# Turning the first batch's K, Q and P on TensorE instead of on VectorE and by DMA

## The chip, the cores and the metric

The kernel runs on one core of a Trainium2 chip. The metric is device time in microseconds for one execution, taken as the median of several runs. The profile is one execution, recorded by the hardware profiler. Engines are named as in the profile: PE is TensorE, PEld its weight loads, DVE is VectorE, ACT is ScalarE, POOL is GpSimd, SP is SyncE, which here only issues transfers.

## What is computed

Block-causal attention over 8 batches, 8 heads, 576 positions and 64 channels a head, and then a feed-forward layer on the 4608 rows of 512 values.

```python
scores = scale * np.matmul(q, k.transpose(0, 1, 3, 2))
mask = block_i >= block_j          # blocks of 64 positions
scores = np.where(mask, scores, -1000000000.0)
attn = np.exp(scores - np.max(scores, axis=-1, keepdims=True))
attn = attn / (np.sum(attn, axis=-1, keepdims=True) + 1e-09)
x = np.matmul(attn, v)             # then heads side by side: 4608 x 512
h = np.maximum(np.maximum(x @ w1, x @ w2), x @ w3)   # 512 -> 768
return h @ w_out                                     # 768 -> 512
```

All of it is in float32.

## The kernel before

Attention works by pairs of heads (class `Pair`, four pairs a batch, with two `Head` objects each). The feed-forward layer works by chunks (class `Chunk`): a batch's 576 rows are cut in half 0 (256) and half 1 (320). Its products at line 919 use operands split in a high and a low part of type fp32r, three products for one; the weights are split the same way on the chip. Class `Unit` does that for one weight block of 512 columns: 24 units, each with a transfer issued by POOL, two ScalarE passes (L288 and a cast in the helper at L235), five VectorE passes (`clamp` L294, `shift` L301, `sign` L307, `power` L313, `rest` L324), three products (L331, which is fp32 and shows as two records, L332 and L333), and a last copy.

The first batch is treated apart, so that the feed-forward layer can begin early. It is cut in FRONT pairs, which take queries and keys 0 to 255 (tiles t = 0 and 1 of 128 queries), and BACK pairs, which take queries 256 to 575 (tiles 2 and 3, and the last 64 queries of both heads together as tile 4) against all 576 keys. Later batches use EARLY and WHOLE pairs, with all queries. For a tile t the scores are 128 x 128(t+1).

For one pair the steps are these. `load` fetches K on SP's queue and Q on ScalarE's (SP's in later batches) into the tile `nat`, in four transfers each that put 32x32 blocks where a 32x32 turn wants them (L709). `turn_qk` turns them on VectorE into `kq` (L730 for FRONT, L733 for the others). `qk` makes the scores in PSUM (L749; `qk4` at L756 for tile 4). `top` takes the minimum of the negated scores on VectorE (L406), `exp` the exponential on ScalarE (L499; `exp4` L773), `scale` divides by the sum, on ScalarE (L422) or GpSimd (L424). P must then be turned, as P·V contracts over the keys. `turn` does it by 32x32 blocks on VectorE into `pz` (L522, and L526 for the rest of tile 4), and `move` sends the four quarters of partitions to their place in `pt` by four transfers on SP's queue (L534). `exp` writes in an order that suits this (`by_turns`). `pv` multiplies (L801), and the result is copied (the helper `copy`, L235 on ScalarE, L237 on VectorE) and split in `xh` and `xl` (L240).

The order of all instructions is written out ahead by a planner, `in_order`: every step is a `Job` with a cost on the engines that may do it, a rank, the jobs that it follows and the slots of buffers that it takes and gives back. Each engine takes the ready job of least rank. PSUM tiles named "sb" have five slots, shared by scores and P·V; those named "pm" have three, for the weight conversion and the feed-forward layer.

Of the kernel before, what the change touches and what calls it, by code (L numbers as in the profile page):

```python
# [34 lines left out]
SEND = 620.0  # L35
# [5 lines left out]

GAP = 60.0
SMALL = 130.0
DEBUG = False


class Job:

    def __init__(self, cost, rank, call, after=(), take=(), give=(), lasts=0.0):
        self.cost, self.rank, self.call, self.lasts = cost, rank, call, lasts
        self.take, self.give = list(take), list(give)
        self.next, self.left = [], 0
        for j in after:
            if j is not None:
                j.next.append(self)
                self.left += 1


def in_order(jobs, slots):


    free = {}
    busy = {e: False for e in LAG}
    ready = {e: [] for e in LAG}
    events, seq, out = [], 0, []

    def post(t, kind, job, eng=None):
        nonlocal seq  # L70
        seq += 1
        heapq.heappush(events, (t, seq, kind, job, eng))

    def arrive(t, job, by=None):
        for e in job.cost:
            post(t + (LAG[by][e] if by else 0.0), "ready", job, e)
        if not job.cost:
            post(t + job.lasts, "done", job)

    for n, job in enumerate(jobs):  # L80
        job.n, job.begun = n, False
        if job.left == 0:
            arrive(0.0, job)
    while events:
        t = events[0][0]
        while events and events[0][0] <= t:
            _, _, kind, job, eng = heapq.heappop(events)
            if kind == "ready":
                heapq.heappush(ready[eng], (job.rank, job.n))
            elif kind == "idle":  # L90
                busy[eng] = False
            else:
                for s in job.give:
                    free[s] = free.get(s, slots[s]) + 1
                for nxt in job.next:
                    nxt.left -= 1
                    if nxt.left == 0:
                        arrive(t, nxt, eng)
        for eng, queue in ready.items():
            if busy[eng]:  # L100
                continue
            later = []
            while queue:
                top = heapq.heappop(queue)
                job = jobs[top[1]]
                if job.begun:
                    continue
                if all(free.get(s, slots[s]) >= job.take.count(s) for s in job.take):
                    for s in job.take:
                        free[s] = free.get(s, slots[s]) - 1  # L110
                    job.begun = busy[eng] = True
                    out.append((job, eng))
                    post(t + job.cost[eng], "idle", None, eng)
                    post(t + max(job.cost[eng], job.lasts), "done", job, eng)
# [28 lines left out]
def kernel(  # L143
# [76 lines left out]

    nat = const.tile([P, 2, S], F32, name="nat")

    jobs = []

    def job(cost, rank, call, *args, after=(), take=(), give=(), lasts=0.0):
        j = Job(cost, rank, lambda eng: call(eng, *args), after, take, give, lasts)
        jobs.append(j)
        return j

# [13 lines left out]
    class Unit:  # L243


        def __init__(self, u, src, dst, n, prior, *early, first=None):
# [14 lines left out]
            j = job({}, 0, lambda eng: None, after=(j,), lasts=MOVE)  # L261
# [122 lines left out]
    class Part:  # L384


        def __init__(self, first, later, halves, keys, queries, run, beside=False):
# [7 lines left out]
            self.loads = 1 if keys < S else 2  # L395

    WHOLE = Part(((3,), (2, 0)), (1,), (1, 0), S, slice(0, S), slice(0, RUN), True)
# [28 lines left out]
    class Head:  # L426
# [28 lines left out]
        def turns(self, t0, after):  # L455

            pair, part, self.scales = self.pair, self.pair.part, {}
            for t in part.tiles:
                r = t0 + 8 + t / 2 + (SECOND if part.beside and t in part.later else 0)
                self.scales[t] = job(norm_cost(P * (t + 1)), r, self.scale, t, after=(self.inv[t],))  # L460
            scales, alone = self.scales, part.loads == 2
            self.turned, first = [], None
            if part.last:
# [15 lines left out]
            if alone or self.j:  # L479
                turned = self.turned if alone else self.turned + pair.heads[0].turned  # L480
                self.moved = job(
                    {"SP": 4 * SEND}, t0 + 13, self.move, after=turned, take=("pt",), give=("pz",), lasts=4 * SEND + TURNED
                )
                if not alone:
                    pair.heads[0].moved = self.moved
            return first

        def top(self, eng, t):

# [48 lines left out]
    class Pair:  # L538
# [3 lines left out]
        def __init__(self, b, hp, part, n):  # L542
            self.b, self.hp, self.part = b, hp, part
            self.heads = [Head(self, j) for j in range(2)]
            self.x32, self.o, self.xs, self.ps, self.began = [None, None], {}, {0: [], 1: []}, {}, None

            self.at = 256 * (n % 2) if part.loads == 1 else 0
            self.vn, self.q8 = vns[n % 2].rearrange("p (c h d) -> p c h d", h=2, d=D), q8s[n % 2]

        def plan(self, first, before):  # L550

            part, loads = self.part, {}
            for nm, n, r in (("kn", 4, -15), ("qn", 4, -15), ("vn", 3, -4)):
                e = "ACT" if nm == "qn" and not part.beside else "SP"
                prior = before and before.loads[nm]
                loads[nm] = job(
# [4 lines left out]
                    after=(prior,),  # L561
                    take=(nm,) * (part.loads if nm != "vn" else 1),
                    lasts=n * LOAD + DMA,
                )
            begun.append(loads["kn"])
            n = part.queries.stop - part.queries.start
            tq = job(
                {"DVE": dve(part.keys + n)},
                first - TURN,
                self.turn_qk,  # L570
                after=(loads["kn"], loads["qn"]),
                take=("kq",),
                give=("kn", "qn") * part.loads,
            )

            cost = {ts: 4 * pe(*[P * (t + 1) for t in ts], least=64) for ts in part.groups}
            prior = job(
# [48 lines left out]
            if part.last:  # L626
# [34 lines left out]
        def alone(self, first):  # L661
# [7 lines left out]
                )  # L669
            self.finish(prior, first, priors)  # L670

        def finish(self, prior, r, priors={}):
            self.xjobs = {}
            for half in self.part.halves:
# [14 lines left out]
            join((prior,), ("pt",) * self.part.loads + ("vn",))  # L689

        def values(self, eng):
            for half in self.part.halves:
# [6 lines left out]
        def load(self, eng, nm):  # L699
            src = {"qn": q, "kn": k, "vn": v}[nm]  # L700
            h0 = 2 * self.hp
            if nm != "vn":

                queue = nc.scalar if eng == "ACT" else nc.sync
# [63 lines left out]

        def exp4(self, eng):
            nm, sm, _ = self.stat  # L770
            self.p4 = att.tile([P, S], F32, name="p4", bufs=slots["p4"])
            for a in range(2):
                nc.scalar.activation(  # L773
                    by_turns(self.p4[:, self.of4(a)], False),
                    by_turns(self.ps[a], True),
                    AF.Exp,
                    bias=nm[:, 1:2],
                    scale=-1.0,
# [9 lines left out]
        def inverse4(self, eng):  # L788
            rs = self.stat[2]
            nc.vector.reciprocal(rs[:, 0:1], rs[:, 0:1])  # L790

        def scale4(self, eng):
            normalise(eng, self.p4, self.stat[2][:, 0:1])

        def pv(self, eng, half):

# [282 lines left out]
```

## Time and profile before

| | us |
|---|---|
| median of 3 runs | 936.66 (935.87 to 937.34) |
| the profiled execution, its own time | 936.99 |
| its span | 935.2 |
| TensorE busy | 884.5 |
| VectorE busy | 537.4 |
| ScalarE busy | 469.4 |
| GpSimd busy | 252.0 |

A busy time is the union of an engine's instructions; a releaser in the profile is the instruction that ended a wait, as semaphore events tell it. The granted clock is a share of TensorE's full 2.4 GHz; its lower level is 1.2 GHz, so a stretch at 0.75 is half at the one and half at the other. The span is shorter than the execution by what lies before the first and behind the last instruction, here 1.8 us.

### The profile page before, as it was taken

What the parts mean: (1) busy time and instruction counts of PE and PEld (TensorE: products, weight loads), DVE (VectorE), ACT (ScalarE), POOL (GpSimd) and SP (SyncE); (2) the same over time, 40 slices, a digit from 0 to 9 for tenths busy, and PEclk for the clock granted to TensorE, in tenths of its full rate; (3) what the DMA queues carried; (4) which work ended last, traced back from release to release, by engine and by line L of the source; (5) the groups of instructions that cost most, each with busy time, mean ns of one, the idle gap of its engine ahead of it and who ended that gap; (6) DMA issues with size and microseconds to landing.
All of it is one profiled execution on the core that took longest, in us unless ns stands there. A gap on an engine that the chain in (4) does not pass through costs nothing.

```text
span 935.2 us, 16716 instructions
## 1 busy us (share of the span) xinstructions
PE 884.5 (95%) x5736; PEld 730.2 (78%) x5736; DVE 537.4 (57%) x1571; ACT 469.4 (50%) x1332; POOL 252.0 (27%) x376
## 2 busy tenths in 40 slices
PE   3578987999999999999999999999999999999998
PEld 2246754787787888888888888888888888899997
DVE  5596988687763646556564645565574655431111
ACT  3474565575554554647455555556364555422111
POOL 4342322234322231313231232214131222222201
PEclk9798999999999999999999999999999999999999
DMA  6794455876555555545435555555533553320010
GB/s 137 200 307 95 113 134 137 169 161 138 124 110 127 110 132 109 110 112 117 104 67 128 109 120 109 128 110 123 115 79 88 111 125 81 96 72 24 1 34 23
DMA packets 244693, 104.92 MB, mean 112 GB/s; under 512 B 202112, under 2 KB 236928, under 8 KB 244608
## 3 DMA queue, kind: packets, MB, share of 16 engines
q1 hardware_dynamic: 221952, 88.91, 42.3%
q0 software_dynamic: 3456, 12.58, 4.2%
q10 hardware_dynamic: 19200, 2.36, 1.6%
q8 instruction: 45, 0.74, 0.3%
q14 instruction: 40, 0.33, 0.1%
HBM read 41.94 MB, written 9.44 MB: 55 GB/s over the span
## 4 chain that ended last, share of the span: by engine, by line
PE 86%; DMA 5%; DVE 5%; ACT 2%; issue 1%; SPq 1%; ACTq 0%; DVEq 0%
PE pm L919 48%; PE pm L985 16%; PE sb L801 10%; PE sb L749 8%; PE sb L756 3%; DMA pt<-pz 2%; DMA nat<-in_q_dram 2%; PE pm L331 1%; DVE pz L522 1%; ACT p L499 1%; DMA vn<-in_v_dram 1%; SPq L534 1%; DVE left L324 1%; DVE sb L406 1%; DMA nat<-in_k_dram 0%
## 5 line engine op out<-in xcount | busy, mean ns | idle before, releaser
L919 PE MATMUL pm<-xh,w 128*128 128x320 f32 (+1 forms) x2304 | 496.9, 303 | 2.7 <-ACT w L235 2.1
L919 PEld LDWEIGHTS pm<-xh,w 128*128 128x128 f32 x2304 | 378.5, 190 | 22.5 <-issue 14.1
L919 PE MATMUL pm<-xl,w 128*128 128x256 f32 (+1 forms) x1152 | 340.9, 296 | 1.8 <-POOL xl L240 1.8
L919 PEld LDWEIGHTS pm<-xl,w 128*128 128x128 f32 x1152 | 218.6, 190 | 8.0 <-issue 4.8
L406 DVE CUSTOM_DVE_ANT_0 sb<-sb,mask 128x512 f32<-128x512 f32 (+3 forms) x288 | 144.6, 527 | 124.1 <-PE sb L756 68.9
L934 DVE TENSOR_TENSOR m<-pm,m 128x256 f32<-128x256 f32 (+1 forms) x192 | 87.0, 453 | 163.6 <-PE pm L919 155.3
L522 DVE STREAM_TRANSPOSE pz<-p 128x384 f32<-128x384 f32 (+3 forms) x320 | 156.9, 525 | 21.3 <-ACT p L422 18.1
L499 ACT ACTIVATE p<-sb,nm 128x128 f32<-128x128 f32 (+3 forms) x256 | 134.3, 528 | 67.3 <-DVE nm L406 58.4
L240 POOL TENSOR_TENSOR hl<-m,hh 128x256 fp32r<-128x256 f32 x96 | 71.2, 741 | 320.6 <-ACT hh L235 288.9
L424 POOL TENSOR_TENSOR p<-p,rs 128x384 f32<-128x384 f32 (+4 forms) x132 | 97.8, 762 | 187.2 <-DVE rs L637 174.2
L801 PE MATMUL sb<-pt,vn 128*64 128x320 f32 (+4 forms) x896 | 105.6, 379 | 19.1 <-DMA pt<-pz 16.8
L985 PE MATMUL pm<-wo,hh 128*128 128x512 f32 x384 | 119.9, 392 | 0.9 <-ACT wo L235 0.9
L801 PEld LDWEIGHTS sb<-pt,vn 128*64 128x64 f32 x896 | 63.0, 143 | 60.4 <-issue 19.1
L749 PE MATMUL sb<-kq 64*128 64x256 f32 (+3 forms) x512 | 91.3, 476 | 15.6 <-DVE kq L730 12.5
L235 ACT CAST hh<-m 128x256 fp32r<-128x256 f32 x96 | 38.9, 406 | 124.1 <-DVE m L934 119.2
L422 ACT ACTIVATE p<-p,rs 128x512 f32<-128x512 f32 (+4 forms) x156 | 86.3, 599 | 20.9 <-DVE rs L637 12.3
L240 POOL TENSOR_TENSOR xl<-x,xh 128x256 fp32r<-128x256 f32 (+1 forms) x64 | 51.4, 808 | 156.8 <-ACT xh L235 156.8
L749 PEld LDWEIGHTS sb<-kq 64*128 64x128 f32 x512 | 46.9, 196 | 51.0 <-issue 20.8
L985 PEld LDWEIGHTS pm<-wo,hh 128*128 128x128 f32 x384 | 70.9, 188 | 16.1 <-ACT wo L235 1.7
L985 PE MATMUL pm<-wo,hl 128*128 128x512 f32 x192 | 74.8, 390 | 0.0
L235 ACT COPY m<-pm 128x256 f32<-128x256 f32 (+1 forms) x96 | 38.3, 399 | 41.5 <-PE pm L919 27.8
L235 ACT COPY osb<-pm 128x512 f32<-128x512 f32 x36 | 21.1, 587 | 71.3 <-PE pm L985 71.3
(68 smaller groups left out, 683.6 us busy)
## 6 DMA issues: line engine op xcount, KB each, us to landing
pt<-pz SPq DMA_DIRECT2D x224, 200.0 KB, 4.0
w<-in_moe_w_dram POOLq DMA_DIRECT2D x18, 512.0 KB, 6.9
nat<-in_k_dram SPq DMA_DIRECT2D x128, 72.0 KB, 2.4
vn<-in_v_dram SPq DMA_DIRECT2D x64, 128.0 KB, 2.4
out_dram<-osb SPq DMA_DIRECT2D x32, 256.0 KB, 2.0
nat<-in_q_dram SPq DMA_DIRECT2D x96, 72.0 KB, 2.6
pt<-pz SPq DMA_DIRECT2D x32, 152.0 KB, 4.4
wo<-in_moe_w_out_dram POOLq DMA_DIRECT2D x6, 512.0 KB, 4.4
```

The costliest lines, as they stand in the source:

```text
L235: nc.scalar.copy(dst, src)
L240: {"DVE": nc.vector, "POOL": nc.gpsimd}[eng].tensor_tensor(out=dst, in0=a, in1=b, op=ALU.subtract)
L406: nc.vector.tensor_tensor_reduce(out=ps, in0=ps, in1=hidden, scale=-SCALE, scalar=first, op0=ALU.add, op1=ALU.min, accum_out=out_)
L422: nc.scalar.mul(p, p, r)
L424: nc.gpsimd.tensor_tensor(out=p, in0=p, in1=r.broadcast_to([P, p.shape[1]]), op=ALU.mult)
L499: nc.scalar.activation(by_turns(self.p[t], False), by_turns(self.ps.pop(t), True), AF.Exp, bias=nm[:, c : c + 1], scale=-1.0, accum_out=sm ...
L522: nc.vector.transpose(dst, p[:, 0 : n * P])
L749: nc.tensor.matmul(ps, self.q[h.own, P * t : P * (t + 1)], self.k[h.own, 0:w], start=True, stop=True)
L801: nc.tensor.matmul(o[h.own].rearrange("p (i u) -> p i u", u=n)[:, :, c0 : c0 + z - a], self.vn[:, kt, h.j, :], h.pt[:, :, h.off + a : h.of ...
L919: nc.tensor.matmul(self.ps, w[i, f][:, c, :], xx, start=(c == 0 and s == 0), stop=(c == NC - 1 and s == 2))
L934: nc.vector.tensor_tensor(out=m, in0=ps, in1=m, op=ALU.max)
L985: nc.tensor.matmul(self.po[: self.rows], h, w[f], start=(f == 0 and s == 0), stop=(f == NF - 1 and s == 2))
```

## The change

For FRONT and BACK pairs, which are the first batch alone, the turns go to TensorE. `load` fetches K and Q in natural order (position on the partition, both heads' channels side by side in a run of 128 columns, so runs of 64 floats) into 128x128 chunks of the same tile `nat`: two transfers for 128-row chunks of the two heads, and a third for the last 64 positions. `raise_qk` turns each chunk by a 128x128 transpose on TensorE into an "sb" tile of PSUM, and `place_qk` copies from there into `kq`, on ScalarE or VectorE as the planner picks. For P, `exp` writes in natural order, `raise_p` (and `raise4` for tile 4, whose last 64 columns GpSimd first copies beside themselves) turns by the same transpose, and `place` and `place4` copy into `pt` in the order that `pv` reads. No `pz` and no `move` is left in the first batch. The later batches keep their steps.

The planner gets a new property of a job, `moved`: the time that its transfer takes on a single DMA resource, which the planner fills in sequence (`landing`). It is given to the weight loads, to K, Q and V, and to the moves, of all batches; so orders may differ in the later batches as well.

```diff
+RAISE = 215.0
...
-    FRONT = Part(((1, 0),), (), (0,), 256, slice(0, 256), slice(0, 96))
-    BACK = Part(((3,), (2,)), (), (1,), S, slice(256, S), slice(96, RUN))
+    FRONT = Part(((1, 0),), (), (0,), 256, slice(0, 256), slice(0, 96), plain=True)
+    BACK = Part(((3,), (2,)), (), (1,), S, slice(256, S), slice(96, RUN), plain=True)
...
+            if part.plain:
+                return self.plain_turns(t0)
...
+        def plain_turns(self, t0):
+            pair, part = self.pair, self.pair.part
+            heads = pair.heads
+            shared = part.loads == 1 and self.j
+            gate = heads[0].gate if shared else None
+            first = heads[0].placed[0] if shared else None
+            self.placed = []
+            def place(call, *args, n, after):
+                j = job(
+                    {"ACT": act(n), "DVE": dve(n)},
+                    t0 + 12,
+                    call,
+                    *args,
+                    after=(after, first or (self.placed[0] if self.placed else None)),
+                )
+                self.placed.append(j)
+                return j
+            for t in part.tiles:
+                up = job(
+                    {"PE": RAISE * (t + 1)},
+                    t0 + 12,
+                    self.raise_p,
+                    t,
+                    after=(self.scales[t], gate),
+                    take=("sb",) if gate else ("sb", pair.tag),
+                )
+                gate = self.gate = gate or up
+                join((up,), (f"p{t}",))
+                join((place(self.place, t, n=P * (t + 1), after=up),), ("sb",))
+            if part.last:
+                if self.j == 0:
+                    pair.raised = [
+                        job({"PE": RAISE * n}, t0 + 12, pair.raise4, a, after=(pair.scaled, gate), take=("sb",))
+                        for a, n in ((0, 4), (1, 1))
+                    ]
+                    join(pair.raised, ("p4",))
+                for a, n in ((0, 256), (1, 64)):
+                    place(self.place4, a, n=n, after=pair.raised[a])
+                if self.j == 1:
+                    for a in range(2):
+                        join([h.placed[-2 + a] for h in heads], ("sb",))
+            self.moved = join(self.placed, ())
+            self.first = None
+            return None
+        def raise_p(self, eng, t):
+            p = self.p[t]
+            z = psa.tile([P, P * (t + 1)], F32, name="sb")
+            for c in range(t + 1):
+                nc.tensor.transpose(z[:, c * P : c * P + P], p[:, c * P : c * P + P], plus.bitcast(F32))
+            self.ps[t] = z
...
+        def place(self, eng, t):
+            a, step, u = PLACE[t]
+            n = t + 1
+            a += self.off + u + 32 - step
+            dst = self.turned_p()[:, :, a : a + step * n].rearrange("p i (k u) -> p k i u", u=step)[:, :, :, step - 32 :]
+            copy(eng, dst, self.ps.pop(t).rearrange("p (k i c) -> p k i c", i=4, c=32))
...
+            dst, src = self.p[t], self.ps.pop(t)
+            if not self.pair.part.plain:
+                dst, src = by_turns(dst, False), by_turns(src, True)
             nc.scalar.activation(
-                by_turns(self.p[t], False), by_turns(self.ps.pop(t), True), AF.Exp, bias=nm[:, c : c + 1], scale=-1.0, accum_out=sm[:, c : c + 1]
+                dst, src, AF.Exp, bias=nm[:, c : c + 1], scale=-1.0, accum_out=sm[:, c : c + 1]
             )
...
+            if part.plain:
+                tq = self.plain_qk(first - TURN, loads)
+            else:
...
+        def plain_qk(self, rank, loads):
+            part, o = self.part, self.at // P
+            if part.loads == 1:
+                banks = ((((o, o + 1, 4 + o, 5 + o), ((0, 0, 256),)),))
+            else:
+                a = part.queries.start // P
+                own = tuple(range(a, 4))
+                banks = [((4, 5, 6, 7), ((0, 2, 512),))]
+                if a:
+                    banks.append(((*own, 8), ((0, 1, P * len(own)), (P * len(own), 0, 64))))
+                else:
+                    banks += [(own, ((0, 1, 512),)), ((8,), ((0, 0, 64),))]
+            ups, downs = [], []
+            for n, (chunks, copies) in enumerate(banks):
+                up = job(
+                    {"PE": RAISE * len(chunks)},
+                    rank,
+                    self.raise_qk,
+                    n,
+                    chunks,
+                    after=(loads["kn"], loads["qn"]),
+                    take=("sb", "sb5") + (("kq",) if n == 0 else ()),
+                ) if n == 0 else job(
+                    {"PE": RAISE * len(chunks)}, rank, self.raise_qk, n, chunks, after=(ups[0], loads["kn"], loads["qn"]), take=("sb", "sb5")
+                )
+                ups.append(up)
+                put = []
+                for c0, which, w in copies:
+                    m = w if which else 2 * w
+                    put.append(job({"ACT": act(m), "DVE": dve(m)}, rank + 1, self.place_qk, n, c0, which, w, after=(up, *downs[:1])))
+                    downs.append(put[-1])
+                join(put, ("sb", "sb5"))
+            join(ups, ("kn", "qn") * part.loads)
+            return join(downs, ())
+        def raise_qk(self, eng, n, chunks):
+            z = self.ps["qk", n] = psa.tile([P, P * len(chunks)], F32, name="sb")
+            for c, x in enumerate(chunks):
+                nc.tensor.transpose(z[:, c * P : c * P + P], chunk[:, x], plus.bitcast(F32))
...
+            if nm != "vn" and self.part.plain:
+                queue = nc.scalar if eng == "ACT" else nc.sync
+                own, c0 = (self.part.queries, 0) if nm == "qn" else (slice(0, self.part.keys), 4)
+                n = min(own.stop, 512)
+                a, z = (self.at + own.start) // P, (self.at + n) // P
+                for j in range(2):
+                    queue.dma_start(
+                        chunk[:, c0 + a : c0 + z, 64 * j : 64 * j + 64],
+                        src[self.b, h0 + j, own.start : n, :].rearrange("(c p) d -> p c d", p=P),
+                    )
+                if own.stop == S:
+                    p0 = 0 if nm == "qn" else 64
+                    queue.dma_start(
+                        chunk[p0 : p0 + 64, 8].rearrange("p (h d) -> p h d", h=2),
+                        src[self.b, h0 : h0 + 2, 512:S, :].rearrange("h p d -> p h d"),
+                    )
+                return
...
+        def raise4(self, eng, a):
+            z = self.ps[a] = psa.tile([P, P if a else 512], F32, name="sb")
+            for c in range(1 if a else 4):
+                src = self.p4[:, c * P : c * P + P]
+                if a:
+                    src = self.p4[:, 512:640]
+                nc.tensor.transpose(z[:, c * P : c * P + P], src, plus.bitcast(F32))
         def scale4(self, eng):
-            normalise(eng, self.p4, self.stat[2][:, 0:1])
+            rs = self.stat[2][:, 0:1]
+            normalise(eng, self.p4[:, 0:S], rs)
+            if self.part.plain:
+                nc.gpsimd.tensor_copy(self.p4[:, S:640], self.p4[:, 512:S])
```

## Rows read from the trace of the kernel before

**Rows 1.** Busy time by stretch: busy us (x count) per engine, clock, DMA share, GB/s

```profile
0.00:80.00 80.00, 45.08 (x179) 25.29 (x180) 51.42 (x151) 39.28 (x109) 31.04 (x50) 0.85 0.74 195
80.00:160.00 80.00, 71.04 (x378) 48.83 (x379) 72.83 (x176) 48.09 (x116) 22.36 (x26) 0.96 0.55 133
160.00:935.00 775.00, 768.39 (x5183) 656.05 (x5181) 413.11 (x1246) 382.05 (x1109) 198.60 (x302) 1.00 0.45 102
```

**Rows 2.** TensorE's waits, 0 to 160 us: us in total, times, longest

```profile
PE sb L801 <- DMA pt<-pz: 15.7, 4, 8.3
PE sb L749 <- DVE kq L730: 12.5, 3, 5.4
PE sb L749 <- DVE rs L633: 3.2, 1, 3.2
```

**Rows 3.** The chain of waits, 100 to 165 us: start, us, what

```profile
121.21 5.63 DMA pt<-pz
```

**Rows 4.** Busy time by shorter stretches

```profile
5.00:26.00 21.00, 10.04 (x44) 6.38 (x44) 13.03 (x54) 10.22 (x35) 7.64 (x12) 1.00 0.72 168
26.00:35.00 9.00, 0.70 (x4) 0.32 (x4) 1.23 (x3) 0.74 (x2) 0.48 (x1) 0.61 0.91 268
...
80.00:120.00 40.00, 38.88 (x238) 29.31 (x238) 40.00 (x88) 24.14 (x54) 14.69 (x17) 1.00 0.53 122
```

**Rows 5.** VectorE's groups by line, 0 to 160 us: busy, mean ns, idle before

```profile
L522 DVE STREAM_TRANSPOSE pz<-p 128x512 f32<-128x512 f32 (+3 forms) x42 | 22.0, 536 | 0.8 <-POOL p L424 0.8
L307 DVE SCALAR_TENSOR_TENSOR wo<-w,wo 128x512 int32<-128x512 int32 x18 | 13.3, 745 | 0.0
...
L730 DVE STREAM_TRANSPOSE kq<-nat 128x512 f32<-128x512 f32 x4 | 2.8, 698 | 4.6 <-DMA nat<-in_q_dram 4.6
...
L526 DVE STREAM_TRANSPOSE pz<-p 128x128 f32<-128x128 f32 x10 | 2.7, 266 | 0.0
```

**Rows 6.** Groups by line and shape, whole span

```profile
L235 ACT COPY osb<-pm 128x512 f32<-128x512 f32 x36 | 21.1, 587 | 71.3 <-PE pm L985 71.3
...
L235 ACT COPY m<-pm 128x256 f32<-128x256 f32 x48 | 17.8, 372 | 21.0 <-PE pm L919 18.9 <-POOL hl L240 0.9
...
L240 POOL TENSOR_TENSOR left<-m,left 128x64 fp32r<-128x64 f32 x48 | 15.5, 323 | 0.0
...
L733 DVE STREAM_TRANSPOSE kq<-nat 128x896 f32<-128x896 f32 x4 | 4.4, 1102 | 9.0 <-DMA vn<-in_v_dram 9.0
...
L237 DVE COPY x<-sb 128x320 f32<-128x320 f32 x6 | 2.9, 490 | 13.2 <-PE sb L801 13.2
```

**Rows 7.** DMA issues, 0 to 160 us: count, KB each, median us to landing

```profile
pt<-pz SPq DMA_DIRECT2D x32, 152.0 KB, 4.4
...
pt<-pz SPq DMA_DIRECT2D x16, 96.0 KB, 2.5
```

**Rows 8.** Tiles pt and nat, issues on SP: ns min/median/max

```profile
L534 SPq DMA_DIRECT2D pt<-pz x51: 542/603/1390, 15.1 to 164.4; - x51
...
L709 SPq DMA_DIRECT2D nat<-in_k_dram x44: 312/452/1413, 0.7 to 150.9; - x44
```

**Rows 9.** SP's issues in order of time: start, us, what

```profile
51.37 9.95 SPq L534 DMA_DIRECT2D pt<-pz  x8
61.83 1.22 SPq L718 DMA_DIRECT2D vn<-in_v_dram  x2
```

**Rows 10.** The chain of waits, 0 to 300 us, pieces on TensorE

```profile
77.48 1.93 PE pm L331 x2
...
87.73 0.86 PE pm L331 x2
...
97.20 1.44 PE pm L919 x12
```

**Rows 11.** VectorE's waits, 0 to 160 us

```profile
DVE kq L733 <- DMA vn<-in_v_dram: 9.0, 1, 9.0
```

**Rows 12.** TensorE in order of time, 55 to 60 us

```profile
58.85 1.55 PE L801 MATMUL sb<-pt,vn 128*64 128x256 f32 x8
```

More of the change, by code (lines that the diff above doesn't have):

```diff
@@ L43, with __init__ @@
 SMALL = 130.0
+RAISE = 215.0
 DEBUG = False
 class Job:
-    def __init__(self, cost, rank, call, after=(), take=(), give=(), lasts=0.0):
-        self.cost, self.rank, self.call, self.lasts = cost, rank, call, lasts
+    def __init__(self, cost, rank, call, after=(), take=(), give=(), lasts=0.0, moved=0.0):
+        self.cost, self.rank, self.call, self.lasts, self.moved = cost, rank, call, lasts, moved
         self.take, self.give = list(take), list(give)
@@ L77, in arrive, with landing @@
         if not job.cost:
-            post(t + job.lasts, "done", job)
+            post(landing(t, job), "done", job)
+    def landing(t, job):
+        nonlocal moving
+        t1 = t + job.lasts
+        if job.moved:
+            moving = max(moving, t) + job.moved
+            t1 = max(t1, moving + DMA)
+        return t1
     for n, job in enumerate(jobs):
@@ L113, in in_order @@
                     post(t + job.cost[eng], "idle", None, eng)
-                    post(t + max(job.cost[eng], job.lasts), "done", job, eng)
+                    post(max(t + job.cost[eng], landing(t, job)), "done", job, eng)
                     break
@@ L221, with job @@
     nat = const.tile([P, 2, S], F32, name="nat")
+    chunk = nat.rearrange("p a s -> p (a s)").rearrange("p (c n) -> p c n", n=P)
     jobs = []
-    def job(cost, rank, call, *args, after=(), take=(), give=(), lasts=0.0):
-        j = Job(cost, rank, lambda eng: call(eng, *args), after, take, give, lasts)
+    def job(cost, rank, call, *args, after=(), take=(), give=(), lasts=0.0, moved=0.0):
+        j = Job(cost, rank, lambda eng: call(eng, *args), after, take, give, lasts, moved)
         jobs.append(j)
@@ L260, in __init__ @@
             )
-            j = job({}, 0, lambda eng: None, after=(j,), lasts=MOVE)
+            j = job({}, 0, lambda eng: None, after=(j,), lasts=MOVE, moved=1600.0)
             j = self.sized = job({"ACT": act(512, False)}, rank, self.size, after=(j,), take=self.temps)
@@ L384, with __init__ @@
     class Part:
-        def __init__(self, first, later, halves, keys, queries, run, beside=False):
+        def __init__(self, first, later, halves, keys, queries, run, beside=False, plain=False):
             self.first, self.later = first, later
@@ L481, in turns @@
                 self.moved = job(
-                    {"SP": 4 * SEND}, t0 + 13, self.move, after=turned, take=("pt",), give=("pz",), lasts=4 * SEND + TURNED
+                    {"SP": 4 * SEND}, t0 + 13, self.move, after=turned, take=("pt",), give=("pz",), lasts=4 * SEND + TURNED, moved=9.0 * RUN
                 )
@@ new lines, in raise_p, with turned_p @@
+        def raise_p(self, eng, t):
[4 more added lines that the diff above has]
+            self.ps[t] = z
+        def turned_p(self):
+            if not hasattr(self, "pt"):
+                pair = self.pair
+                if self.j and pair.part.loads == 1:
+                    self.pt = pair.heads[0].pt
+                elif pair.tag == "pt":
+                    self.pt = att.tile([P, 4, RUN], F32, name="pt", bufs=slots["pt"])
+                else:
+                    z = att.tile([P, 4 * (RUN + 16)], F32, name="pz", bufs=slots["pz"])
+                    self.pt = z[:, 0 : 4 * RUN].rearrange("p (i u) -> p i u", i=4)
+            return self.pt
@@ new lines, in place, with place4 @@
+        def place(self, eng, t):
[4 more added lines that the diff above has]
+            copy(eng, dst, self.ps.pop(t).rearrange("p (k i c) -> p k i c", i=4, c=32))
+        def place4(self, eng, a):
+            step = PLACE[4][1]
+            n = 1 if a else 4
+            at = PLACE[4][0] + (288 if a else 0)
+            src = self.pair.ps[a].rearrange("p (k i h c) -> p k i h c", i=4, h=2, c=16)[:, :, :, self.j]
+            if a:
+                dst, src = self.turned_p()[:, :, at : at + 16], src[:, 0]
+            else:
+                at += 16 - step
+                dst = self.turned_p()[:, :, at : at + step * n].rearrange("p i (k u) -> p k i u", u=step)[:, :, :, step - 16 :]
+            copy(eng, dst, src)
@@ L552, in plan @@
             part, loads = self.part, {}
-            for nm, n, r in (("kn", 4, -15), ("qn", 4, -15), ("vn", 3, -4)):
+            n = 4 if not part.plain else 3 if part.last else 2
+            for nm, n, r in (("kn", n, -15), ("qn", n, -15), ("vn", 3 if part.last else 2, -4)):
                 e = "ACT" if nm == "qn" and not part.beside else "SP"
@@ L563, in plan @@
                     lasts=n * LOAD + DMA,
+                    moved=1200.0 * part.keys / S if part.plain or nm == "vn" else 1400.0,
                 )
             begun.append(loads["kn"])
[L566 to L574, printed above, removed]
+            if part.plain:
+                tq = self.plain_qk(first - TURN, loads)
+            else:
+                n = part.queries.stop - part.queries.start
+                tq = job(
+                    {"DVE": dve(part.keys + n)},
+                    first - TURN,
+                    self.turn_qk,
+                    after=(loads["kn"], loads["qn"]),
+                    take=("kq",),
+                    give=("kn", "qn") * part.loads,
+                )
             cost = {ts: 4 * pe(*[P * (t + 1) for t in ts], least=64) for ts in part.groups}
@@ L625, in plan @@
             join([x for h in self.heads for x in h.scales.values()], ("stat",))
-            if part.last:
+            if part.last and not part.plain:
                 join([h.turned[0] for h in self.heads], ("p4",))
@@ new lines, in raise_qk, with place_qk @@
+        def raise_qk(self, eng, n, chunks):
+            z = self.ps["qk", n] = psa.tile([P, P * len(chunks)], F32, name="sb")
+            for c, x in enumerate(chunks):
+                nc.tensor.transpose(z[:, c * P : c * P + P], chunk[:, x], plus.bitcast(F32))
+        def place_qk(self, eng, n, c0, which, w):
+            if not hasattr(self, "q"):
+                self.kq = att.tile([P, 2, S], F32, name="kq", bufs=slots["kq"])
+                self.q, self.k = self.kq[:, 0], self.kq[:, 1]
+            z, part = self.ps["qk", n], self.part
+            if which:
+                a = part.queries.start if which == 1 else 0
+                copy(eng, self.kq[:, which - 1, a : a + w], z[:, c0 : c0 + w])
+                return
+            a = 512 if w == 64 else 0
+            copy(eng, self.kq[:, :, a : a + w], z[:, c0 : c0 + 2 * w].rearrange("p (a s) -> p a s", a=2))
@@ L688, in finish @@
                 )
-            join((prior,), ("pt",) * self.part.loads + ("vn",))
+            join((prior,), (self.tag,) * self.part.loads + ("vn",))
         def values(self, eng):
@@ L770, in exp4 @@
             nm, sm, _ = self.stat
-            self.p4 = att.tile([P, S], F32, name="p4", bufs=slots["p4"])
+            self.p4 = att.tile([P, 640], F32, name="p4", bufs=slots["p4"])
             for a in range(2):
+                dst, src = self.p4[:, self.of4(a)], self.ps[a]
+                if not self.part.plain:
+                    dst, src = by_turns(dst, False), by_turns(src, True)
                 nc.scalar.activation(
-                    by_turns(self.p4[:, self.of4(a)], False),
-                    by_turns(self.ps[a], True),
+                    dst,
+                    src,
                     AF.Exp,
```

9 lines of the change are left out of this document (added).

## The prediction

> **What bounds the kernel now.** I read first the busy times of three stretches side by side. From 160 us on TensorE is busy for 768.4 of 775 us [rows 1]: the later part of the kernel is TensorE's own work, with 6.6 us left to win there whatever the rest does. The batch that the change edits lies before that, together with the conversion of the 24 weight blocks and chunk 0. There TensorE is busy 45.1 + 71.0 = 116.1 of 160 us, so it is idle for 43.9 us. It also works in part at its lower level: the granted clock is 0.85 in the first 80 us and 0.96 in the next 80 [rows 1], which I price at 45.1 × 0.15 + 71.0 × 0.04 = 9.6 us (estimate: busy time times the missing share of clock). So 53.5 us of TensorE time are lost in the first 160 us, nearly all that a change of the first batch can win.
>
> The view of TensorE's waits says for what it stood idle: 15.7 us for the moves pt<-pz (four times, 8.3 us the longest), 12.5 us for turned keys and queries (5.4 us of it is the first load), 3.2 us behind a small VectorE instruction [rows 2], and the remaining 12.6 us in short waits for weight blocks and x. The chain of waits shows such a move on the path late too, 5.63 us at 121 us [rows 3]. VectorE is the second bound: it is busy for 40.0 of 40 us from 80 to 120 us [rows 4], and for 124.2 of the first 160 [rows 1].
>
> **What is removed.** For batch 0, VectorE loses four turns of K and Q of 512 columns and four of 896 (2.8 and 4.4 us), 40 turns at L522 (2 heads × 2 tiles × 4 FRONT pairs, 2 × 3 × 4 BACK pairs; 40 × 0.536 = 21.4 us) and eight at L526 (8 × 0.266 = 2.1) [rows 5, 6]: 30.7 us. SP's queue loses all 48 issues of pt<-pz of that batch (16 of 96 KB, 32 of 152 KB, 6.4 MB [rows 7]), 0.603 us each [rows 8], so 29 us. What stands behind them on that queue moves up: from 51.37 us eight such issues held it for 9.95 us, and the load of V that followed was issued only at 61.83 [rows 9]. The loads of K and Q go from four issues to two (FRONT) or three (BACK) each, with runs of 256 bytes in place of 128: 12 issues fewer on SP and 12 on ScalarE's queue, by SP's 0.452 us [rows 8] 5 us of each, and fewer packets in the stretch from 26 to 35 us, when DMA is at 0.91 share and every engine nearly idle [rows 4].
>
> **What is added on TensorE.** Each 128x128 turn is one transpose. A FRONT pair has 4 for K and Q and 2 × 3 for P, so 10; a BACK pair 7 for K and Q, 2 × 7 for P and 5 for the last tile, so 26. Four of each make 144. The trace has no transpose. Nearest is L331, an fp32 product with the same 128x128 identity: two records, 0.86 us for 512 columns at the full level, so 0.215 us for 128 columns; the same pair took 1.93 us at the lower level, 0.48 for 128 [rows 10]. The other end is a product that passes once: L919 does twelve of 256 columns in 1.44 us, 0.06 for 128 [rows 10]. I take 0.215, from the row with this dtype: 144 × 0.215 = 31.0 us (ends 8.6 and 69).
>
> The Trainium skill, "TensorE: Matmul & The Clock Gate", has two rules that differ here. Its Terms say that the transpose mode is 4 times faster for FP32; by that the sum would be near 31 / 4 = 7.8 us, an estimate by that page. Its Part 4 (PE-mode transpose) gives about 275 ns for a transpose in one kernel's context, which speaks against this change: 144 × 0.275 = 39.6 us by it. No run here shows either yet; both have their rival below.
>
> **What is added elsewhere.** Copies out of PSUM: a FRONT pair has one of 512, two of 256 and two of 128 columns; a BACK pair 512, 256, 128, and twice 512, 384, 256, 64. ScalarE copies 256 columns in 0.372 us and 512 in 0.587, VectorE 320 in 0.490 [rows 6]. On a straight line through ScalarE's two (0.157 + 0.00084 a column) that is 1.86 and 4.52 us a pair, 25.5 us in all; on VectorE, by 0.490 against 0.426 us on that line, 29.3. The planner may put each on either; I halve them: VectorE 124.2 − 30.7 + 14.7 = 108.2 us, ScalarE 39.3 + 48.1 [rows 1] + 12.8 = 100.2 of 160. Both stay below TensorE's new 147.1. The exp now writes the same columns in natural order; I price that at nothing, since ScalarE has 60 us spare; without that cover 56 instructions at an assumed 0.1 us either way are ±5.6 us, of which little would reach TensorE. GpSimd's four extra copies of 64 columns cost about 0.323 us each [rows 6], 1.3 us, under its idle time (it is busy 53 of 160 us [rows 1]). The planner's new due times for transfers alter only orders; after 160 us I give that ±2 us, for the 6.6 us there.
>
> **Where the new wait stands.** A transpose of K and Q now waits on TensorE for its load, where VectorE waited before (9.0 us once, until a landing [rows 11]). Behind it in TensorE's order stand conversions and products of chunk 0. That costs nothing where TensorE was idle at the same time, as it was in that wait (8.3 us of it [rows 2]). If a load is late while TensorE has other work, the whole lateness is paid.
>
> **The sum.** The stretch ends later by the added 31.0 us, and earlier by what is filled of the 53.5. What stays lost I estimate as: 5.4 us to the first load; half of the 11.0 us of idle between 5 and 26 us (21 − 10.0 [rows 4]), as FRONT's chain keeps its steps and has only 8.6 us of transposes to fill it, 5.5; 3 of the 9.6 us of low clock; and a quarter of the 12.6 us of short waits, 3.2, since the weight blocks come sooner from a VectorE with 16 us less to do. The waits for the moves and the later turns I count as gone. That leaves 17.1, and 31.0 + 17.1 − 53.5 = −5.4 us. The profiled execution took 936.99 us, 1.8 over its span of 935.2; less 5.4 it is 931.6, and from the median of 936.66 it is 931.3. The weak term is what stays lost: with 12 us the result is 926, with 24 it is 938.
>
> **Rivals.**
> *Transposes cost little.* If a transpose passes once (0.06 us), 22.4 us less of TensorE's time are added. All of it would give 909, but the weight blocks would then set the pace on VectorE, which keeps 108.2 us of work. I let half through: 931.3 − 11.2 = 920. For it speaks that data are only moved; against it that the trace's fp32 products with this identity take two slow records.
> *TensorE waits for PSUM.* Each group of turns needs one of the five "sb" banks until its copy is done: 5 groups in a FRONT pair (1 + 4), 8 in a BACK pair (2 + 4 + 2), 52 in all, shared with scores and P·V. A copy of 0.26 to 0.59 us stands in order behind VectorE's weight steps of up to 0.745 us [rows 5]. At 0.25 us a group TensorE waits 13 us more, and the time is 944, slower than before. It decides from 5.4 / 52 = 0.10 us a group. For it: VectorE is full from 80 to 120 us, where BACK pairs run; against: ScalarE can take the copies, and is busy 24 of those 40 us [rows 4].
> *Transposes cost more.* If a quarter of them run at the lower level, the mean is 0.75 × 0.215 + 0.25 × 0.48 = 0.28 us, 9.4 us more: 941. Part 4 named above points to this size as well.
> *Nothing is won.* TensorE is idle only 9.0 us between 80 and 160 us [rows 1], and BACK's transposes are 104 × 0.215 = 22.4 us; if these stay there, they use up what FRONT wins: 936.7.
>
> **How the numbers follow.** Chances: forecast 0.45 (own range 926 to 938), cheap transposes 0.27 (914 to 927), PSUM waits 0.15 (938 to 950), dear transposes 0.08, nothing won 0.05. About 0.2% (1.9 us) is what a measurement of this kernel can tell from no change. Faster: 0.36 of the forecast's 0.45 and the 0.27 of cheap transposes, 0.63. Same: 0.06 of the forecast, the 0.05, and 0.01 of the dear ones, 0.12. Slower: the rest, 0.25. The range of 914 to 944 leaves out the far half of the PSUM case and the full gain of cheap transposes.
>
> **What would show it.** TensorE: 144 (or 288) new records and 0.215 us a turn; no wait on pt<-pz before the second batch; the fourth P·V of FRONT well before 58.85 us [rows 12]; TensorE's idle time of the first 160 us down from 43.9 to below 20. VectorE's busy time before 160 us near 108 us. Wrong would be: turns at 0.06 to 0.1 us; waits of TensorE on copies (tile sb, ScalarE or VectorE) of over 5 us in sum; a new wait for nat loads ahead of the transposes; or a stretch after 160 us that loses more than 2 us by another order.

## The result

The changed kernel takes 928.34 us (median of 4 runs, 927.53 to 929.03) against 936.33 us before: a ratio of 0.9913, 95% interval 0.9896 to 0.9930, so 8 us faster. The forecast was 931.3 us, and faster.

The busy times of the same three stretches as [rows 1], of the changed kernel:

```profile
0.00:80.00 80.00, 61.15 (x307) 40.07 (x308) 64.73 (x176) 53.25 (x142) 31.64 (x50) 0.96 0.60 173
80.00:160.00 80.00, 74.25 (x425) 53.02 (x424) 62.40 (x164) 50.23 (x131) 21.34 (x28) 0.98 0.43 99
160.00:925.00 765.00, 760.03 (x5151) 651.57 (x5149) 402.97 (x1219) 376.10 (x1088) 193.34 (x299) 1.00 0.45 100
```

TensorE is idle for 160 − 61.15 − 74.25 = 24.6 us before 160 us, where it was 43.9, and its clock is 0.96 and 0.98 where it was 0.85 and 0.96. After 160 us little is idle in either (5.0 us here, 6.6 before). So the time of the kernels below follows from one number, the work that TensorE still has at 160 us: 760.0 us here and 768.4 before. The 8.4 us between them are most of the 9.5 us by which the span fell (925.7 against 935.2). What a span has beyond 160 us and that work is 4.5 to 7.4 us in every run but one (10.8 with the moves put back).

TensorE's waits in the same 160 us, beside [rows 2]:

```profile
PE sb L824 <- DMA nat<-in_k_dram: 4.8, 1, 4.8
PE pm L346 <- ACT w L249: 4.3, 3, 2.7
PE sb L1000 <- ACT p L606: 2.5, 1, 2.5
PE sb L986 <- POOL p L440: 2.0, 1, 2.0
PE sb L933 <- DVE kq L251: 2.0, 2, 1.1
...
PE sb L558 <- DVE pz L251: 1.6, 2, 1.0
PE sb L824 <- ACT p L606: 1.4, 2, 0.9
PE sb L558 <- DVE pt L251: 1.4, 1, 1.4
...
PE sb L558 <- DVE kq L251: 0.4, 1, 0.4
```

No wait for pt<-pz is left (15.7 us before), the later waits of the scores for turned K and Q are down from 12.5 − 5.4 = 7.1 to 2.7 us (the 2.0 shown and 0.7 behind ScalarE's copies), and nothing new is long: the 4.8 us is the first load. The transposes stand at L558 (P), L824 (K and Q) and L986 (tile 4). Two pieces of the changed kernel's timeline, TensorE alone (start, us, what), and the view by line of the transposes of P (ns min/median/max):

```profile
96.89 0.93 PE L824 MATMUL sb<-plus,nat 128*128 128x128 f32 x7
```

```profile
49.49 1.07 PE L1000 MATMUL sb<-pt,vn 128*64 128x256 f32 x8
```

```profile
L558 PE MATMUL sb<-plus,p x80: 270/273/478, 15.5 to 133.0; 128*128 128x128 f32 x80
```

A transpose is one record. Its own duration is 0.273 us, but seven in a row take 0.93 us, so they start (0.93 − 0.273) / 6 = 0.11 us apart, about half of the 0.215 that I took from [rows 10]. The last FRONT P·V begins at 49.49 us, where it began at 58.85 [rows 12].

### The profile page after: what moved, and what is told of

The parts are those of the page before. It is cut to its first block, busy times and chain, and to the rows that moved or that the text cites. A ratio compares the mean times of both kernels' runs of the same rounds, so it can differ in the third digit from the quotient of the medians.

```text
span 925.7 us, 16909 instructions
## 1 busy us (share of the span) xinstructions
PE 895.4 (97%) x5880; PEld 744.7 (80%) x5880; DVE 530.1 (57%) x1555; ACT 479.6 (52%) x1359; POOL 246.3 (27%) x377
## 4 chain that ended last, share of the span: by engine, by line
PE 90%; DVE 5%; ACT 1%; issue 1%; DMA 1%; POOL 1%; ACTq 0%; SPq 0%; DVEq 0%; POOLq 0%
PE pm L1118 49%; PE pm L1184 16%; PE sb L1000 10%; PE sb L933 9%; PE sb L940 3%; PE pm L345 1%; DVE sb L422 1%; DVE wo L321 1%; DVE wo L308 1%; DVE left L338 1%; POOL p L440 1%; DMA nat<-in_q_dram 1%; PE sb L558 0%; ACT w L249 0%; DVE wo L315 0%
## 5 line engine op out<-in xcount | busy, mean ns | idle before, releaser
L629 DVE STREAM_TRANSPOSE pz<-p 128x512 f32<-128x512 f32 (+1 forms) x280 | 136.4, 525 | 21.8 <-ACT p L438 20.0
L440 POOL TENSOR_TENSOR p<-p,rs 128x384 f32<-128x384 f32 (+4 forms) x129 | 90.0, 719 | 186.7 <-DVE rs L750 180.8
L438 ACT ACTIVATE p<-p,rs 128x512 f32<-128x512 f32 (+4 forms) x159 | 89.6, 608 | 20.2 <-DVE rs L750 12.9
L1000 PE MATMUL sb<-pt,vn 128*64 128x320 f32 (+4 forms) x840 | 90.4, 362 | 4.0 <-ACT p L606 2.5
L933 PE MATMUL sb<-kq 64*128 64x256 f32 (+3 forms) x512 | 88.5, 466 | 2.6 <-DVE kq L251 2.0
L1000 PEld LDWEIGHTS sb<-pt,vn 128*64 128x64 f32 x840 | 55.3, 137 | 37.4 <-issue 5.0
```

What stands on the lines that cost most here:

```text
L438: nc.scalar.mul(p, p, r)
L440: nc.gpsimd.tensor_tensor(out=p, in0=p, in1=r.broadcast_to([P, p.shape[1]]), op=ALU.mult)
L629: nc.vector.transpose(dst, p[:, 0 : n * P])
L933: nc.tensor.matmul(ps, self.q[h.own, P * t : P * (t + 1)], self.k[h.own, 0:w], start=True, stop=True)
L1000: nc.tensor.matmul(o[h.own].rearrange("p (i u) -> p i u", u=n)[:, :, c0 : c0 + z - a], self.vn[:, kt, h.j, :], h.pt[:, :, h.off + a : h.of ...
```

## The experiments

Each was timed in at least five runs beside runs of the kernel before on the same chip (medians of 937.4 to 939.5 us there), so ratios to before are the safer comparison. The changed kernel's own is 0.9913. "Idle" is TensorE's idle time before 160 us and "left" its busy time after, both in the profiled execution, which took 938.04 us in the last run.

| run | us | ratio (95%) | idle | left |
|---|---|---|---|---|
| before | 936.33 | 1 | 43.9 | 768.4 |
| changed | 928.34 | 0.9913 (0.9896 to 0.9930) | 24.6 | 760.0 |
| old turns, new due times | 922.19 | 0.9840 (0.9818 to 0.9861) | 33.1 | 755.9 |
| new turns, old due times | 921.72 | 0.9839 (0.9815 to 0.9863) | 21.4 | 754.1 |
| changed, transpose planned at 110 ns | 920.11 | 0.9820 (0.9799 to 0.9841) | 19.2 | 753.2 |
| P alone | 927.52 | 0.9880 (0.9851 to 0.9908) | 27.1 | 760.7 |
| K and Q alone | 924.21 | 0.9854 (0.9823 to 0.9884) | 32.3 | 755.4 |
| FRONT alone | 929.55 | 0.9909 (0.9880 to 0.9937) | 28.8 | 761.5 |
| BACK alone | 929.94 | 0.9906 (0.9879 to 0.9933) | 30.3 | 761.4 |
| changed, fp32 products | 931.35 | 0.9938 (0.9916 to 0.9959) | 15.0 | 761.6 |
| changed, moves put back | 971.94 | 1.0357 (1.0330 to 1.0384) | 50.8 | 798.5 |
| changed, VectorE's turns put back | 944.98 | 1.0072 (1.0049 to 1.0094) | 34.7 | 777.2 |
| before, small cost 140 | 930.48 | 0.9916 (0.9895 to 0.9936) | 40.9 | 765.0 |
| before, delay 265 | 934.56 | 0.9960 (0.9941 to 0.9979) | 42.3 | 768.8 |

**Turns and due times apart.** The change has two parts that can be had alone: the turns, and the planner's due times (`moved`). First the due times on the old turns:

```diff
--- before
-            post(t + job.lasts, "done", job)
+            post(landing(t, job), "done", job)
+
+    def landing(t, job):
+
+        nonlocal moving
+        t1 = t + job.lasts
+        if job.moved:
+            moving = max(moving, t) + job.moved
+            t1 = max(t1, moving + DMA)
+        return t1
...
-            j = job({}, 0, lambda eng: None, after=(j,), lasts=MOVE)
+            j = job({}, 0, lambda eng: None, after=(j,), lasts=MOVE, moved=1600.0)
...
-  give=("pz",), lasts=4 * SEND + TURNED
+  give=("pz",), lasts=4 * SEND + TURNED, moved=9.0 * RUN
...
+                    moved=1200.0 * part.keys / S if nm == "vn" else 1400.0,
```

> The kernel before with nothing but the planner's new due times for transfers, so other orders and the same instructions. Theory A (the turns themselves bring the gain): within 2 us of before, 934 to 939. Rival B (the orders that the planner now finds bring it): most of the 8 us, 928 to 931.

922.19 us: more than the whole change brings, with every turn still on VectorE and every move on DMA. Rival B held. The waits of TensorE before 160 us in this run:

```profile
PE sb L760 <- DVE kq L741: 14.6, 4, 5.7
PE sb L760 <- DVE kq L744: 4.2, 1, 4.2
...
PE sb L812 <- DMA nat<-in_k_dram: 2.6, 1, 2.6
...
PE sb L812 <- DMA pt<-pz: 0.8, 1, 0.8
```

The wait for the moves is 0.8 us, where it was 15.7. Not all of that is won: the waits for turned K and Q are 14.6 + 4.2 = 18.8 us, where they were 12.5, and TensorE's idle time as a whole fell from 43.9 to 33.1 us. The moves themselves did not get faster (a median of 5.5 and 3.0 us to landing, against 4.4 and 2.5 [rows 7]):

```profile
pt<-pz SPq DMA_DIRECT2D x32, 152.0 KB, 5.5
...
pt<-pz SPq DMA_DIRECT2D x16, 96.0 KB, 3.0
```

The planner now puts other work ahead of them. TensorE's timeline shows it at the second FRONT P·V. In the kernel before, that P·V stands ahead of the first BACK pair's scores and holds TensorE for 8.3 us:

```profile
34.57 1.55 PE L801 MATMUL sb<-pt,vn 128*64 128x256 f32 x8 [8.30 <-DMA pt<-pz]
...
38.13 3.81 PE L749 MATMUL sb<-kq 64*128 64x512 f32 x8
```

With the new due times the scores go first, after a wait of 4.23 us for K and Q, and the P·V finds its operand there:

```profile
32.35 3.36 PE L760 MATMUL sb<-kq 64*128 64x512 f32 x8 [4.23 <-DVE kq L744]
35.87 1.55 PE L812 MATMUL sb<-pt,vn 128*64 128x256 f32 x8 [0.16 <-ACT p L509]
```

Then the turns with the old due times:

```diff
--- changed
-        if job.moved:
+        if False:
```

> The changed kernel with the planner's old due times, so the turns on TensorE in another order. Theory A: within 2 us of the changed kernel, 926 to 930. Rival B: most of the gain is lost, 933 to 937.

921.72 us. Each part alone brings 15 us, and both together bring 8. So the gain isn't a sum of parts, and neither theory holds for this run: it is faster than both expected.

**The planned cost of a transpose.**

```diff
--- changed
-RAISE = 215.0
+RAISE = 110.0
```

> The changed kernel with the planner's cost of a transpose at the measured 110 ns in place of 215. Theory A: orders matter little, within 2 us of the changed kernel, 926 to 930. Rival B: an order made with the true cost brings 3 us or more, below 925.

920.11 us, the fastest of all; the work is that of the changed kernel. Rival B's number held. The interval lies clear of the changed kernel's and overlaps those of the two runs above. Whether the truer cost or the luck of an order did it stays open, as the last pair of runs shows what an order alone can do.

**One part of the turns alone.** Two flags in place of one choose P's turns (`plain`) and the turns and loads of K and Q (`raw`) for each part:

```diff
--- changed
-    FRONT = Part(..., plain=True)
-    BACK = Part(..., plain=True)
+    FRONT = Part(..., plain=True, raw=False)   # P alone; K and Q alone: False, True
+    BACK = Part(..., plain=True, raw=False)    # FRONT alone: True, True and False, False
```

> P alone is turned on TensorE, K and Q are loaded and turned on VectorE as before. Theory A1 (the moves of P were the wait that ended last, 15.7 of 43.9 us): most of the gain, 929 to 932. Rival A2 (K and Q's turn and loads count as much): 932 to 935.

> K and Q alone are turned on TensorE, P is turned on VectorE and moved by DMA as before. Theory A1: little, 934 to 937. Rival A2: 3 us or more, 930 to 934.

> Only the FRONT pairs turn on TensorE, BACK pairs as before. Theory D (the gain lies before 80 us, where TensorE's idle time fell from 34.9 to 18.9 us, as chunk 0 can begin earlier): most of the gain, 928 to 932. Rival E (BACK's moves at 73, 127 and 151 us are what is won): 933 to 937.

> Only the BACK pairs turn on TensorE, FRONT pairs as before. Theory D: under 3 us won, 934 to 937. Rival E: most of the gain, 928 to 932.

These don't tell the parts apart: all four gain 0.9 to 1.5%, P alone and K and Q alone more than either theory gave them, and FRONT as much as BACK. If the parts' gains were their own, FRONT and BACK would add up to some 17 us. All four also have the new due times. Beside the old turns with these (0.9840), FRONT alone and BACK alone are slower, and the intervals of P alone and of K and Q alone overlap with it: none is clearly faster. The due times don't take away every wait for a move, either: with K and Q alone TensorE still stands 6.8 us for them.

```profile
PE sb L1000 <- DMA pt<-pz: 6.8, 2, 4.9
```

Each was planned anew, so each has another order on every engine. I had taken such runs for clean cuts, and they aren't.

**Same order, one cost changed.** Three edits are made behind the planner, so the order of the changed kernel stands. First, twice TensorE's work in the turns:

```diff
--- changed
-                nc.tensor.transpose(z[:, c * P : c * P + P], chunk[:, x], plus.bitcast(F32))
+                nc.tensor.matmul(z[:, c * P : c * P + P], chunk[:, x], plus.bitcast(F32), start=True, stop=True)
... the same in raise_p and raise4
```

> The changed kernel in the same order with each transpose replaced by an fp32 product with the identity, two records of 0.215 us in sum, where the trace of the changed kernel shows 0.11 us a transpose: 144 x 0.105 = 15 us more work for TensorE. Theory A with TensorE as the bound of the whole first 160 us: 10 to 15 us slower than the changed kernel, 938 to 943. Rival C (the chain of each pair and VectorE are the bound there, TensorE has room): under 6 us slower, 929 to 934.

```profile
97.82 1.72 PE L824 MATMUL sb<-plus,nat 128*128 128x128 f32 x14
```

Fourteen records in 1.72 us are 0.11 apart, so a turn takes 0.22 us: 144 × 0.11 = 16 us of work more. The kernel takes 931.35 us; by the ratios (0.9938 against 0.9913) that is 2.3 us more, and the intervals overlap. TensorE's idle time before 160 us fell from 24.6 to 15.0 us in its place, and its clock rose from 0.96 and 0.98 to 0.98 and 1.00 in the two stretches. Rival C held: in this order most of what is added to TensorE goes into waits that are there anyhow, and a part may be paid back by the clock.

Second, the transfers of P, in place:

```diff
--- changed
+        def moved_on(self):
...
+            if first.put == 4:     # the last copy of a FRONT pair's or a BACK head's P
...
+                for i in range(4):
+                    piece = self.turned_p()[32 * i : 32 * i + 32, :, run]
+                    nc.sync.dma_start(piece, piece)
...
             copy(eng, dst, self.ps.pop(t).rearrange("p (k i c) -> p k i c", i=4, c=32))
+            self.moved_on()
... the same behind the copy of place4
```

> The changed kernel in its own order on TensorE, VectorE and ScalarE, with the 48 transfers of P put back behind the copies: the same bytes from and to the same place, issued on SP, and P·V waits for them. Theory A (P's way through DMA was the wait that counted; here the planner does not know of it): 5 us or more slower than the changed kernel, 933 to 945. Rival G (the gain was SP's order and the planner's, and other work covers a transfer): within 3 us, 926 to 931.

```profile
PE sb L1011 <- DMA pz<-pz: 20.4, 5, 7.5
PE sb L1011 <- DMA pt<-pt: 13.4, 3, 7.9
```

Their transfers, 0 to 200 us (count, KB each, median us to landing):

```profile
pz<-pz SPq DMA_DIRECT2D x16, 152.0 KB, 4.2
pt<-pt SPq DMA_DIRECT2D x16, 152.0 KB, 4.4
...
pz<-pz SPq DMA_DIRECT2D x8, 96.0 KB, 3.6
...
pt<-pt SPq DMA_DIRECT2D x8, 96.0 KB, 2.2
```

971.94 us, 4.5% over the changed kernel by the ratios. TensorE waits 33.8 us for these transfers before 160 us, and its clock falls to 0.87 and 0.91. Theory A held, and by more than I gave it. By the ratios it is some 42 us for 12 moves, so 3.5 us each, with what the lower clock costs: in an order that does not allow for it, a move costs about what one of its four transfers takes to land. That is not its price in the kernel before, whose order allowed for the moves and waited 15.7 us for them.

Third, VectorE's turns, of a constant, which nobody reads:

```diff
--- changed
+    def turn_spare(*sizes):
+        for n in sizes:
+            nc.vector.transpose(spare[:, 0:n], mask[:, 0:n])   # called in raise_p, raise_qk, raise4
```

> The changed kernel in its own order, with 30 us of VectorE turns put back that nobody reads, at the places where TensorE now turns (at most 480 columns each, of a constant tile). Theory H (VectorE sets the pace of the first 160 us, so its relief is what pays): 8 us or more slower than the changed kernel, 936 to 950. Rival A (the waits for the moves pay, VectorE has room): under 4 us slower, 926 to 932.

```profile
0.00:80.00 80.00, 58.23 (x269) 35.93 (x269) 68.14 (x194) 47.18 (x129) 27.66 (x46) 0.96 0.60 167
80.00:160.00 80.00, 67.06 (x375) 46.49 (x376) 68.59 (x160) 45.77 (x111) 21.13 (x27) 0.94 0.34 79
```

944.98 us. VectorE's busy time over the whole span rises by 23.5 us (530.1 to 553.6, where I had put 30), and the kernel by 1.6% by the ratios, some 15 us. Theory H held: in this order, which was planned without these turns, about two thirds of VectorE's time counts. Before 160 us VectorE's busy time rises only from 127.1 to 136.7 us, as the stretch as a whole is drawn out; 777.2 us are left for TensorE at 160 us.

**An order without a meaning.** Two runs of the kernel before with a planner's constant moved by a few per cent:

```diff
--- before
-SMALL = 130.0
+SMALL = 140.0
```

```diff
--- before
-TO_PE = 250.0
+TO_PE = 265.0
```

> The kernel before with one of the planner's costs, that of a small VectorE instruction, at 140 ns in place of 130: another order without a meaning, the same instructions. Theory A: within 2 us of before, 934 to 939. Rival K (the order of before is a poor one by chance, and nearly any other is better): 4 us or more faster, below 933.

> The kernel before with the planner's delay towards TensorE at 265 ns in place of 250: a second order without a meaning. Theory A: 934 to 939. Rival K: below 933. The spread of this run, the one before and the kernel before says how much of any change of a few us can be order alone.

930.48 and 934.56 us. The first gains 0.84%, as much as the change does (0.87%), with the same work (a few scalings and copies go to another engine), though the constant has nothing to do with transfers. Rival K held for it. The second's 934.56 us lie in Theory A's range, but by the ratio it is 0.4% faster than before, with an interval clear of 1. The waits for the moves are still there, 11.3 us in the first:

```profile
PE sb L749 <- DVE kq L730: 15.3, 3, 6.4
PE sb L801 <- DMA pt<-pz: 11.3, 3, 8.1
```

## Why the prediction came out right, and where it did not

The sign and the size held (8.0 us against 5.4 forecast), but the working holds only in part, and the size came out near by luck.

*The moves and VectorE.* Right as mechanisms, and shown in one order: the waits for pt<-pz are gone from the trace, they cost some 42 us when put back, and VectorE's turns some 15. (VectorE's busy time fell by 7.3 us over the span, 537.4 to 530.1, where I had 16. By the view by line its turns sum to 30.4 us less, its copies of K, Q and P to 16.5 more and its other groups to 3.7 more; the rest I did not trace. Before 160 us, where I expected 108 us, it is busy for 127.1, more than the 124.2 before: other work moved up into the stretch.) Wrong was to book the step "The waits for the moves ... I count as gone" to the turns alone. The due times by themselves took these waits from 15.7 to 0.8 us, by order. I had given the due times "±2 us", for the stretch after 160 us alone; of their 15 us most lie before it, as TensorE has 12.5 us less left at 160 us (755.9 against 768.4).

*The term on TensorE.* "I take 0.215": measured 0.11, so 144 × 0.11 = 15.8 us in place of 31.0. The row with the same dtype was the wrong neighbour, as a transpose is one record and the product two. The Trainium skill, "TensorE: Matmul & The Clock Gate", Terms, has the transpose mode 4 times faster for FP32, and does not say than what; beside the fp32 product it is 2 times here (0.11 us in the changed kernel, 0.22 for the product in the same order). The 275 ns of its Part 4, where the one type named is bf16, are near the 0.273 us of one fp32 record; in a row these start 0.11 us apart, so that figure is no price for many.

*What stays lost.* "That leaves 17.1": measured 24.6 us idle and 61.15 × 0.04 + 74.25 × 0.02 = 3.9 us of low clock, 28.5. (Both this and the 9.6 us before leave out a slow start for which the view gives 1.00; see the last section.) With the true 15.8 the sum of the prediction's form is 15.8 + 28.5 − 53.5 = −9.2 us, near the 9.5 of the span. So the two terms erred by 15 and 11 us in opposite directions, and the forecast was near for that reason, which is luck. The form itself is at fault as well: it lets a microsecond added to TensorE count in full, and the run with fp32 products shows 2.3 of 16.

*The rivals.* PSUM waits did come, in part. The transposes of P (L558) waited 1.6 + 1.4 + 0.4 = 3.4 us for copies. As I read the other waits on tile sb, the transposes of K and Q waited 1.4 us and a P·V (L1000) 2.5 us for a bank that an exponential still read. That is 7.3 us for a bank, where the kernel before has one such wait:

```profile
PE sb L756 <- ACT p L499: 1.6, 1, 1.6
```

The rise of 5.7 us is just over the 5.4 from which I let this rival decide. With the 2.7 us of the scores behind copies of K and Q, the waits on copies alone are 6.1 us, over the 5 us that I had named as a sign of being wrong. It did not decide, since TensorE's idle time fell by 19 us all the same. VectorE took 38 of the copies and ScalarE 26, near the halves that I assumed. Dear transposes and a lost gain did not happen. Cheap transposes did, at half the price and not a quarter, without the further gain that I tied to them.

*What stays open.* Whether the turns as such beat the old kernel. With the old due times, three orders of the old turns take 936.3, 930.5 and 934.6 us and one of the new takes 921.7; with the new due times the old turns take 922.2, and two orders of the new 928.3 and 920.1. The best order with the old turns and the best with the new differ by 0.2% (0.9840 against 0.9820), and their intervals overlap. A wider set of orders for both would be needed; it was not tried.

## What to carry to other kernels

Where a planner writes the order out, a few edited instructions give another order everywhere, and one run of each side compares two orders as much as two kernels: move a constant that means nothing first, and see how far the time goes. To price one cost, change it behind the planner, with the order held. And a wait for a transfer on the critical path may shrink when the planner is told when the transfer lands, before any work is moved to another engine: here it did in one order (15.7 to 0.8 us), and less in another (6.8).

## What the runs showed of the hardware

An fp32 transpose of 128x128 on TensorE is one record of 0.273 us, and a row of them starts 0.11 us apart; an fp32 product with the identity is two records 0.11 us apart each. The first four transposes, from 4.80 us, took 1.12 us, where four at 48.96 us took 0.60, and the longest record of K and Q is 0.476 us, against a median of 0.273. The scores are slow there too:

```profile
6.59 1.65 PE L933 MATMUL sb<-kq 64*128 64x256 f32 x8 [0.68 <-ACT kq L249]
...
22.30 0.92 PE L933 MATMUL sb<-kq 64*128 64x256 f32 x8
```

In the run with the transpose planned at 110 ns eight such products still take 1.65 us at 22.92 us:

```profile
22.92 1.65 PE L933 MATMUL sb<-kq 64*128 64x256 f32 x8
```

The view by stretches gives a granted clock of 1.00 for all of this, so that figure is not to be trusted for the first 20 to 30 us. For the first 80 us as a whole it is lower where TensorE is idle for longer, 0.85 with 34.9 us idle before and 0.96 with 18.9 in the changed kernel. The sum of idle time does not settle it, though: the old turns with new due times and BACK alone have 0.89 and 0.96 with nearly the same 25.8 and 25.7 us idle.
